# Softmax denominators in four timed steps, and head-row copies of parity 1 on another queue

## The chip, the cores and the metric

The kernel runs on one core of a Trainium2 chip. The core has a matrix engine (TensorE, PE in the profile), a vector engine (VectorE, DVE), an engine for activation functions (ScalarE, ACT), a general engine (GpSimd, POOL) and a synchronisation engine (SyncE, SP) that here only issues transfers. [...] The metric is the device time of the kernel in microseconds, as the median of its runs.

## The reference, cut to what matters

The input has 2048 tokens of width 512. It is normalised once, and two branches work on the result. Branch A is attention over a dilated window: each token looks at itself and at 7 earlier tokens, two apart. It has 32 heads of width 16. Branch B mixes neighbouring tokens between two matrix products and then runs a two-layer network with a hidden width of 1376. The output joins them.

```python
def _A_ref(x, wqkv, wo):
    H = 32; Dh = D // H
    W, dil = 8, 2
    q, k, v = ...                       # x @ wqkv, split by head
    off = jnp.arange(W) * dil           # tokens s, s-2, ..., s-14
    logits = einsum("bhsd,bhswd->bhsw", q, kg) * Dh ** -0.5
    attn = softmax(masked logits)
    o = einsum("bhsw,bhswd->bhsd", attn, vg)
    return o @ wo                       # heads merged

def _B_ref(x, w1, w2, w3, w4):
    h = gelu(layernorm(x) @ w1)
    hs = shifted(h) @ w2                # quarters shifted by -1, +1, -2, +2 tokens
    x1 = x + hs
    h2 = gelu(layernorm(x1) @ w3) @ w4
    return x1 + h2

xn = layernorm(x)
out = x + _A_ref(xn) * silu(_B_ref(xn))
```

Since a token sees only tokens of its own parity, the kernel treats the even and the odd tokens as two sequences of 1024, called parity 0 and parity 1.

## The kernel before

The parts of attention and of the network are woven together. Attention runs in 9 units of up to 128 queries for each parity. `attend(n)` handles unit n (0 to 8 are parity 0, 9 to 17 are parity 1): it computes scores for its own unit, weights the values of the unit before, and calls the functions listed in `groups[n]` and `late[n]`. Between the two parities the product with w3 (line 453) runs over four chunks of 512 tokens; the product with w4 (line 473) is woven into parity 1.

The softmax weights are not divided before the product with v. Each value tile has columns of constants beside the 16 value columns of a head, so the product also gives the denominators. Three units form a run, and the results of a run are normalised together. The denominators lie on few partitions, so they take a way through DRAM: `den_d` is written, read back as `dn` over all 128 partitions, inverted, written to `rden_d`, and read back with every value repeated for the 16 rows of its head.

```python
def spread(p, lo, hi):                     # copies head rows to tiles beside mask rows
    for w in range(2):
        for e in range(2):
            for gr in range(4):
                r = 32 * gr + DH * e
                nc.sync.dma_start(                                     # line 250
                    out=(kT, qT)[w][e][r : r + DH, :, lo:hi], in_=kq[p][w][r : r + DH, :, lo:hi]
                )

def ln3_norm(c, a=0, b=TPC):               # normalises chunk c, then turns it
    ...
            nc.vector.tensor_scalar(...)                               # line 431
    nc.sync.dma_start(out=x1n_dram[...], in_=xn3)                      # line 437
    nc.sync.dma_start_transpose(out=x1nT[c], in_=x1n_dram[...])        # line 440

def weighted_out(p, u, op):
    nc.vector.tensor_copy(out=orw[p][...], in_=op[...])                # line 554, empties o_ps
    if u == runs[p][r][1] - 1:
        normalise(p, r)

def normalise(p, r):
    nc.sync.dma_start(out=den_d..., in_=orw[p][DH : P : 32]...)        # line 567
    dn = small.tile([P, n], BF16, name="dn", tag="dn")
    nc.sync.dma_start(out=dn, in_=den_d...)                            # line 573
    rrs[p, r] = (dn, rden_d)

def pack(p, r):                            # 8 copies by GpSimd        # line 581
    ...

def normalise_mid(p, r):
    nc.vector.reciprocal(out=rb, in_=dn)                               # line 592
    nc.sync.dma_start(out=rden_d..., in_=rb)                           # line 593
    ...
    nc.sync.dma_start(out=rr, in_=rden_d...to_broadcast(...))          # line 598

def normalise_end(p, r):
    nc.vector.tensor_tensor(out=oT[p]..., in0=oT[p]..., in1=rr..., op=ALU.mult)   # line 603

late[3].append(lambda: ln3_norm(0))
late[7].append(lambda: ln3_norm(1))
for p in range(2):
    for r, (_, end, _, _) in enumerate(runs[p]):        # end is 3, 6, 9
        n = p * NU + end
        if n + 1 < 2 * NU and not (p == 0 and n >= N1):
            late[n].append(lambda p=p, r=r: pack(p, r))
            late[n + 2].append(lambda p=p, r=r: normalise_mid(p, r))
            if r == 0:
                late[n + (5 if p == 0 else 4)].append(lambda p=p, r=r: normalise_end(p, r))
late[4].append(lambda: spread(1, 0, CUT))

for n in range(N1):                        # parity 0
    attend(n)
for c in range(NCH):                       # product with w3, chunk by chunk
    for a in range((NF + 1) // 2):
        w3_pair(c, a)
        if c == 0 and a == 0:
            weighted(*prev)()              # last unit of parity 0
            ln3_stats(2); ln3_norm(2)
            ln3_stats(3); ln3_norm(3)
            load_w4()
            spread(1, CUT, M)
            pack(0, 2)
        if c == 1 and a == 0:
            normalise_end(0, 1)
            normalise_mid(0, 2)
        if c == 2 and a == 0:
            normalise_end(0, 2)
for n in range(N1, 2 * NU):                # parity 1, with the product with w4
    attend(n)
...
```

Four lines of the w4 stage come up later. Line 479 (VectorE) adds the w4 result to the residual and empties its PSUM tile. Lines 499 and 503 compute and empty the next value tile, and line 524 (ScalarE) takes the exponential of the scores. In the last stage `final_tile` multiplies with wo (line 620) and joins the two branches (lines 626 and 628).

Of the kernel before, what the change touches and what calls it, by code (L numbers as in the profile page):

```python
# [15 lines left out]
def kernel(  # L16
# [14 lines left out]
    nc = tc.nc  # L31
    P = 128
    S = 2048
    D = 512
    H = 32
# [24 lines left out]
    runs = []  # L60
# [20 lines left out]
    def at(kb, n, m):  # L81
        ar, o = (arenas[0], int(kb * KB)) if kb < 164 else (arenas[1], int((kb - 176) * KB))
        return ar[:, o : o + n * m].rearrange("p (n m) -> p n m", n=n)
# [40 lines left out]
    for c in range(NCH):  # L124
        p, k = c // 2, c % 2
        n = 1 if c == 0 else 2
        for t0 in range(k * TPC, (k + 1) * TPC, n):
            nc.sync.dma_start(
                out=xn[p][:, t0 : t0 + n, :],
                in_=xv[p, t0 * P : (t0 + n) * P, :].rearrange("(i q) d -> q i d", q=P),  # L130
# [14 lines left out]
    def load_w4():  # L145
        nc.sync.dma_start(
            out=w4_sb[:, 0 : NF - 1, :],
            in_=B_w4[0 : (NF - 1) * P, :].rearrange("(ft q) n -> q ft n", q=P),
        )
        nc.sync.dma_start(out=w4_sb[0:FL, NF - 1, :], in_=B_w4[(NF - 1) * P : F, :])  # L150
# [91 lines left out]
                    out=(kT, qT)[w][e][:, :, cs], in_=mask[:, w, cs].unsqueeze(1).to_broadcast([P, ND, CH])  # L242
                )

    def spread(p, lo, hi):
        for w in range(2):
            for e in range(2):
                for gr in range(4):
                    r = 32 * gr + DH * e
                    nc.sync.dma_start(  # L250
                        out=(kT, qT)[w][e][r : r + DH, :, lo:hi], in_=kq[p][w][r : r + DH, :, lo:hi]
                    )

# [15 lines left out]
    def layer_stats(src, name, lo=0, hi=TPC):  # L269
        n = hi - lo  # L270
        st = small.tile([P, n, nc.vector.BN_STATS_DIM], F32, name=name + "s", tag=f"{name}s{n}", bufs=2)
        mv = small.tile([P, n, nc.vector.BN_AGGR_DIM], F32, name=name + "m", tag=f"{name}m{n}", bufs=8 if n == 1 else 4)
        for j in range(n):
            nc.vector.bn_stats(out=st[:, j, :], in_=src[:, lo + j, :])
            nc.vector.bn_aggr(out=mv[:, j, :], in_=st[:, j, :])  # L275
        rstd = small.tile([P, n], F32, name=name + "r", tag=f"{name}r{n}", bufs=8 if n == 1 else 4)
        rsqrt_eps(rstd, mv[:, :, 1])
        return mv, rstd
# [143 lines left out]
    def ln3_stats(c, lo=0, hi=TPC):  # L422
        p, k = c // 2, c % 2
        l3.setdefault(c, []).append((lo, hi, *layer_stats(xn[p][:, k * TPC : (k + 1) * TPC, :], "l3", lo, hi)))

    def ln3_norm(c, a=0, b=TPC):
        p, k = c // 2, c % 2
        x_c = xn[p][:, k * TPC : (k + 1) * TPC, :]
        for lo, hi, mv, rstd in l3[c]:
            for j in range(max(lo, a), min(hi, b)):  # L430
                nc.vector.tensor_scalar(
                    out=xn3[:, j, :], in0=x_c[:, j, :], scalar1=mv[:, j - lo, 0:1],
                    scalar2=rstd[:, j - lo : j - lo + 1], op0=ALU.subtract, op1=ALU.mult,
                )
        if b < TPC:
            return
        nc.sync.dma_start(
            out=x1n_dram[c * CH : (c + 1) * CH, :].rearrange("(i q) d -> q i d", q=P), in_=xn3
        )
        nc.sync.dma_start_transpose(out=x1nT[c], in_=x1n_dram[c * CH : (c + 1) * CH, :])  # L440

    def h3(c, ft, n):
# [4 lines left out]
    def w3_pair(c, a):  # L447
        pt = psa("w3_ps")
        fts = [ft for ft in (2 * a, 2 * a + 1) if ft < NF]
        for ft in fts:  # L450
            fs = P if ft < NF - 1 else FL
            for dt in range(ND):
                nc.tensor.matmul(  # L453
                    pt[:fs, ft % 2, :], lhsT=w3_sb[:, dt, ft * P : ft * P + fs], rhs=x1nT[c][:, dt, :],
                    start=(dt == 0), stop=(dt == ND - 1),
                )
        if len(fts) == 2:
            nc.scalar.activation(h3(c, 2 * a, 2), pt, AF.Gelu_apprx_tanh)  # L458
        else:
            nc.scalar.activation(h3(c, NF - 1, 1)[:FL, 0, :], pt[:FL, 0, :], AF.Gelu_apprx_tanh)  # L460
# [100 lines left out]
    rrs = {}  # L561

    def normalise(p, r):
        _, _, ra, rw = runs[p][r]
        den_d = dram.tile([8, ND * rw], BF16, name=f"den_d{p}{r}")
        rden_d = dram.tile([8, ND * rw], BF16, name=f"rden_d{p}{r}")
        nc.sync.dma_start(
            out=den_d.rearrange("(j c) x -> c j x", j=2),
            in_=orw[p][DH : P : 32].rearrange("c j s q -> c j (s q)"),
        )  # L570
        n = H * rw // P
        dn = small.tile([P, n], BF16, name="dn", tag="dn")
        nc.sync.dma_start(out=dn, in_=den_d.rearrange("h (a m) -> (h a) m", a=P // 8))
        rrs[p, r] = (dn, rden_d)

    def pack(p, r):
        _, _, ra, rw = runs[p][r]
        for jj in range(2):
            for cg in range(4):
                hh = 4 * jj + cg  # L580
                nc.gpsimd.dma_start(  # L581
                    out=oT[p][DH * hh : DH * (hh + 1), :, ra : ra + rw],
                    in_=orw[p][32 * cg : 32 * cg + DH, jj],
                )

    def normalise_mid(p, r):
        _, _, ra, rw = runs[p][r]
        n = H * rw // P
        dn, rden_d = rrs[p, r]
        rb = small.tile([P, n], BF16, name="rb", tag="rb")  # L590
        with nc.allow_low_precision("bf16 weights"):
            nc.vector.reciprocal(out=rb, in_=dn)
        nc.sync.dma_start(out=rden_d.rearrange("h (a m) -> (h a) m", a=P // 8), in_=rb)
        if p == 0 and r:
            rr = orws[r % 2][:, 0 : ND * rw]
        else:
            rr = at(rr_at[r % 2] if p else 121, 1, ND * rw)[:, 0, :]
        nc.sync.dma_start(out=rr, in_=rden_d.unsqueeze(1).to_broadcast([8, DH, ND * rw]))
        rrs[p, r] = rr

    def normalise_end(p, r):
        _, _, ra, rw = runs[p][r]
        nc.vector.tensor_tensor(  # L603
            out=oT[p][:, :, ra : ra + rw], in0=oT[p][:, :, ra : ra + rw],
            in1=rrs[p, r].rearrange("p (s q) -> p s q", s=ND), op=ALU.mult,
        )
# [56 lines left out]
    stage_t(1, 0)  # L663
    stage_t(1, 1)
    spread(0, 0, CH)
    mask_fill(1)
    ln_stats(2)
# [9 lines left out]
    for a in (2, 3):  # L677
        qk_pair(1, a)[0]()
    spread(0, CH, M)
    stage_t(2, 0)  # L680
    stage_t(2, 1)
# [22 lines left out]
    N1 = NU  # L704
# [16 lines left out]
    late = {n: [] for n in range(2 * NU + 4)}  # L721

    def st3(n, *ts):
        for t in ts:
            late[n].append(lambda t=t: ln3_stats(t // 4, t % 4, t % 4 + 1))

    st3(1, 0, 1)
    st3(2, 2, 3)
    late[3].append(lambda: ln3_norm(0))
    st3(4, 4, 5)  # L730
    st3(5, 6)
    st3(6, 7)
    late[7].append(lambda: ln3_norm(1))

    w4s = [w4_tile(t) for t in range(S // P)]
    for n in range(N1, 2 * NU):
# [10 lines left out]
    for p in range(2):  # L747
        for r, (_, end, _, _) in enumerate(runs[p]):
            n = p * NU + end
            if n + 1 < 2 * NU and not (p == 0 and n >= N1):  # L750
                late[n].append(lambda p=p, r=r: pack(p, r))
                late[n + 2].append(lambda p=p, r=r: normalise_mid(p, r))
                if r == 0:
                    late[n + (5 if p == 0 else 4)].append(lambda p=p, r=r: normalise_end(p, r))
    CUT = CH
    late[4].append(lambda: spread(1, 0, CUT))

    prev = None

# [25 lines left out]
    for c in range(NCH):  # L785
# [3 lines that stand above are left out]
                weighted(*prev)()  # L789
                prev = None  # L790
                ln3_stats(2)
                ln3_norm(2)
                ln3_stats(3)
                ln3_norm(3)
                load_w4()
                spread(1, CUT, M)
                pack(0, 2)
            if c == 1 and a == 0:
                normalise_end(0, 1)
                normalise_mid(0, 2)  # L800
            if c == 2 and a == 0:
                normalise_end(0, 2)
    load_wo()
    for k in range(2):
# [5 lines left out]
                load_xo(1, k)  # L810
    weighted(*prev)()
    pack(1, 2)
    fq = [(0, i) for i in range(8)]
    gate(8)
    gate(9)
    for t in range(10, 16):
        w4s[t](0, NF)
        final_tile(*fq.pop(0), eng=nc.gpsimd)
        gate(t)
        if t == 11:  # L820
            normalise_end(1, 1)
        if t == 13:
            normalise_mid(1, 2)
    for _ in range(2):
        final_tile(*fq.pop(0), eng=nc.gpsimd)
    for i in (0, 2, 4, 6):
# [37 lines left out]
```

## Time and profile before

| | |
|---|---|
| median of 3 runs | 227.44 us (225.14 to 228.41) |
| span of the profiled execution | 227.5 us |
| TensorE matmul busy | 205.8 us, 90% |
| VectorE busy | 133.5 us, 59% |
| ScalarE busy | 133.1 us, 59% |
| GpSimd busy | 69.4 us, 30% |
| product with w3 (line 453) | from 93.3 to 138.8 us |
| scores of parity 1 begin | 138.9 us |
| last w4 product ends | about 209 us |

A profile of this kind is read from the engine that is nearly always busy, here TensorE: a stretch in which it idles, or runs at a lower clock, is what a change can win. What ended such a stretch is found in the table of waits and in the timelines. Idle time of the other engines costs nothing by itself. A line such as `97.92 0.92 DVE L603 ...` gives the start, the duration, the engine, the line of the kernel, the operation, the tiles written and read, and in brackets the idle time before it and what ended that. Lines with `SPq` are the issues of transfers by SyncE. Transfers that one engine issues wait in one queue: when the front one waits for data, those behind it are not issued.

### The profile page before, as it was taken

Reading aid. Unit: us, or ns where it says so; the run is one execution under the profiler, and the core shown is the slowest. Engines: PE = TensorE matmul, PEld = TensorE weight load, DVE = VectorE, ACT = ScalarE, POOL = GpSimd, SP = SyncE. Lnnn points to the kernel's source line nnn. Section 1 sums busy time; section 2 is a strip of 40 time slices with the busy share of each in tenths; the row PEclk is TensorE's granted clock in tenths of the full one; section 3 lists DMA queues with packets and bytes.
Section 4 is the critical chain, followed back from the end, with each engine's and each line's share of the span. In section 5 each row is a group of like instructions: output and inputs, shape, how many; then the busy total and the mean of one; then the engine's idle time right before and its main releaser. Section 6 shows DMA issues by size and latency. Waiting matters only on the chain.

```text
span 227.5 us, 4995 instructions
## 1 busy us (share of the span) xinstructions
PE 205.8 (90%) x1999; PEld 99.6 (44%) x2028; DVE 133.5 (59%) x242; ACT 133.1 (59%) x162; POOL 69.4 (30%) x139
## 2 busy tenths in 40 slices
PE   8799999999999999939999999299999999999860
PEld 3566455444445544413444444135444544444320
DVE  5859584343969768467340000225666769799991
ACT  2397679588798987613564658428887784221000
POOL 8880532000227236002630000000070162933761
PEclk9999999999999999976999999979999999999995
DMA  5994967969006658235497945790030150401542
GB/s 146 357 331 140 275 104 199 262 102 262 22 0 154 129 92 146 66 105 102 153 202 149 279 63 81 195 320 6 0 69 13 46 101 12 117 3 40 158 140 91
DMA packets 35550, 29.75 MB, mean 131 GB/s; under 512 B 12600, under 2 KB 33432, under 8 KB 35528
## 3 DMA queue, kind: packets, MB, share of 16 engines
q1 hardware_dynamic: 32904, 26.29, 45.4%
q0 software_dynamic: 1536, 2.10, 5.1%
q10 hardware_dynamic: 1088, 1.05, 1.4%
q8 instruction: 16, 0.26, 0.5%
q14 instruction: 6, 0.05, 0.1%
HBM read 12.39 MB, written 4.46 MB: 74 GB/s over the span
## 4 chain that ended last, share of the span: by engine, by line
PE 65%; DMA 10%; DVE 7%; issue 7%; ACT 4%; POOL 3%; SPq 1%; DVEq 0%; ACTq 0%; POOLq 0%
PE w_ps L473 15%; PE w_ps L453 8%; PE qk_ps L362 8%; PE w_ps L391 6%; PE v_ps L499 6%; PE s_ps L519 6%; PE w_ps L414 4%; DMA den_d<-orw 4%; PE qk_ps L378 3%; PE o_ps L542 3%; PE wo_ps L620 3%; ACT arena L524 3%; DVE arena L626 2%; DMA arena<-x1n_dram 2%; DMA rden_d<-rb 2%
## 5 line engine op out<-in xcount | busy, mean ns | idle before, releaser
L524 ACT ACTIVATE arena<-s_ps 128x960 bf16<-128x960 f32 (+2 forms) x72 | 63.1, 934 | 21.5 <-PE s_ps L519 15.1
L581 POOL DMA_DIRECT2D arena<-orw x48 | 24.7, 523 | 71.4 <-DVE orw L554 60.3
L473 PE MATMUL w_ps<-arena 128*128 128x512 bf16 (+1 forms) x154 | 39.4, 385 | 0.7 <-issue 0.2
L458 ACT ACTIVATE arena<-w_ps 128x1024 bf16<-128x1024 f32 x20 | 20.5, 1024 | 22.7 <-PE w_ps L453 22.0
L453 PEld LDWEIGHTS <-arena 128*128 128x128 bf16 (+1 forms) x176 | 18.1, 103 | 26.8 <-issue 7.5
L473 PEld LDWEIGHTS <-arena 128*128 128x128 bf16 (+1 forms) x176 | 16.8, 99 | 20.2 <-issue 1.8
L453 PE MATMUL w_ps<-arena 128*128 128x512 bf16 (+1 forms) x86 | 22.3, 416 | 3.7 <-DVE orw L554 3.6
L499 PE MATMUL v_ps<-wv_sb,arena 128*128 128x512 bf16 (+1 forms) x71 | 19.2, 390 | 4.4 <-DVE arena L479 4.2
L489 DVE SCALAR_TENSOR_TENSOR arena<-sig,arena 128x512 bf16<-128x512 bf16 x16 | 14.7, 926 | 14.2 <-ACT sig L488 14.1
L453 PE MATMUL w_ps<-arena,arena 128*128 128x512 bf16 (+1 forms) x86 | 19.2, 379 | 0.6 <-DMA arena<-x1n_dram 0.4
L554 DVE CAST orw<-o_ps 128x960 bf16<-128x960 f32 (+2 forms) x18 | 19.6, 1091 | 0.0
L488 ACT ACTIVATE sig<-arena 128x512 bf16<-128x512 bf16 x16 | 10.1, 629 | 16.2 <-DVE arena L479 16.2
L519 PEld LDWEIGHTS <-arena 32*128 32x128 bf16 (+1 forms) x576 | 11.8, 94 | 16.7 <-issue 15.8
L418 DVE TENSOR_TENSOR arena<-w_ps,arena 128x512 bf16<-128x512 f32 x16 | 11.0, 688 | 13.6 <-PE w_ps L414 13.6
L266 POOL TENSOR_SCALAR l3r<-l3m 128x1 f32<-128x1 f32 (+1 forms) x10 | 2.2, 224 | 54.9 <-DVE l3m L275 54.9
L519 PE MATMUL s_ps<-arena 32*128 32x120 bf16 (+2 forms) x576 | 18.5, 211 | 0.5 <-ACT arena L524 0.2
L603 DVE TENSOR_TENSOR arena<-arena,orw 128x1440 bf16<-128x1440 bf16 (+1 forms) x2 | 1.7, 836 | 29.0 <-DMA orw<-rden_d 29.0
L362 PE MATMUL qk_ps<-arena 128*128 128x512 bf16 (+1 forms) x95 | 18.2, 343 | 0.2
L628 POOL TENSOR_TENSOR arena<-arena 128x512 bf16<-128x512 bf16 x12 | 14.8, 1244 | 11.8 <-DVE arena L626 10.7
L414 PE MATMUL w_ps<-arena 128*128 128x512 bf16 x55 | 15.6, 381 | 0.6 <-issue 0.2
L503 DVE CAST v_aug<-v_ps 128x512 bf16<-128x512 f32 (+1 forms) x18 | 12.4, 686 | 5.1 <-PE v_ps L499 5.1
L391 PE MATMUL w_ps<-arena 128*128 128x512 bf16 x61 | 14.3, 379 | 0.2
(82 smaller groups left out, 263.4 us busy)
## 6 DMA issues: line engine op xcount, KB each, us to landing
arena<-arena SPq DMA_DIRECT2D x8, 512.0 KB, 6.0
arena<-arena SPq DMA_DIRECT2D x64, 64.0 KB, 2.9
x1n_dram<-arena SPq DMA_DIRECT2D x4, 512.0 KB
arena<-in_A_x_dram SPq DMA_DIRECT2D x4, 512.0 KB, 8.8
arena<-in_A_x_dram SPq DMA_DIRECT2D x6, 256.0 KB, 7.1
arena<-in_B_w_dram SPq DMA_DIRECT2D x1, 1376.0 KB
arena<-in_B_w_dram SPq DMA_DIRECT2D x1, 1280.0 KB
arena<-in_A_wqkv_dram SPq DMA_DIRECT2D x2, 512.0 KB
```

The lines of the kernel that those rows point to most:

```text
L362: nc.tensor.matmul(pt[:, b, hh * w : (hh + 1) * w], lhsT=wqk_sb[:, dt, nt * P : (nt + 1) * P], rhs=xnT[p][:, dt, k * CH + hh * w : k * CH ...
L391: nc.tensor.matmul(pt[:, b, :], lhsT=w1_sb[:, dt, g * P : (g + 1) * P], rhs=xn2T[c][:, dt, :], start=(dt == 0), stop=(dt == ND - 1),)
L414: nc.tensor.matmul(pt, lhsT=w2_src(p, g, m0), rhs=w2_sb[:, g, :], start=(g == 0), stop=(g == ND - 1))
L453: nc.tensor.matmul(pt[:fs, ft % 2, :], lhsT=w3_sb[:, dt, ft * P : ft * P + fs], rhs=x1nT[c][:, dt, :], start=(dt == 0), stop=(dt == ND - 1),)
L458: nc.scalar.activation(h3(c, 2 * a, 2), pt, AF.Gelu_apprx_tanh)
L473: nc.tensor.matmul(pt, lhsT=h3(c, ft, 1)[:fs, 0, jj * P : (jj + 1) * P], rhs=w4_sb[:fs, ft, :], start=(ft == 0), stop=(ft == NF - 1),)
L499: nc.tensor.matmul(vp[:nk, :], lhsT=xnT[p][:, dt, k0 : k0 + nk], rhs=wv_sb[:, dt, :], start=(dt == 0), stop=(dt == ND - 1),)
L519: nc.tensor.matmul(st[:nk, b, i * nq : (i + 1) * nq], lhsT=kT[e][r : r + 32, dt, k0 : k0 + nk], rhs=qT[e][r : r + 32, dt, q0 : q0 + nq], s ...
L524: nc.scalar.activation(prv[:nk, 2 * h : 2 * h + 2], st[:nk, :, 0 : 4 * nq], AF.Exp, scale=SCALE)
L554: nc.vector.tensor_copy(out=orw[p][:, :, :, q0 - ra : q0 - ra + nq], in_=op[:, :, 0 : 4 * nq].rearrange("p j (s q) -> p j s q", q=nq),)
L581: nc.gpsimd.dma_start(out=oT[p][DH * hh : DH * (hh + 1), :, ra : ra + rw], in_=orw[p][32 * cg : 32 * cg + DH, jj],)
L628: eng.tensor_tensor(out=x_o, in0=sg, in1=x_o, op=ALU.add)
```

## The change

The way of the denominators is split into four functions instead of three around the transfers: `normalise` only writes `den_d`, `normalise_dn` reads it back, `normalise_mid` inverts and writes `rden_d`, and `normalise_rr` reads that back repeated. In the same way `ln3_norm` loses its store and its transposed load to `ln3_store` and `ln3_turn`. This lets the program place each issue at a point where its data should already be there, so that the queue of SyncE and VectorE do not stand waiting. Calls that belonged to the last units of parity 0 move into the w3 stage, in a new order. The first half of the head-row copies of parity 1 (`spread(1, 0, CUT)`) moves from SyncE to GpSimd, in two lots of 8.

```diff
-    def spread(p, lo, hi):
-        for w in range(2):
+    def spread(p, lo, hi, q=nc.sync, ws=(0, 1)):
+        for w in ws:
...
-                    nc.sync.dma_start(
+                    q.dma_start(
...
+        ln3_store(c)
+
+    def ln3_store(c):
         nc.sync.dma_start(
             out=x1n_dram[...], in_=xn3
         )
+
+    def ln3_turn(c):
         nc.sync.dma_start_transpose(out=x1nT[c], in_=x1n_dram[...])
...
+        rrs[p, r] = [den_d, rden_d]
+
+    def normalise_dn(p, r):
...
-        nc.sync.dma_start(out=dn, in_=den_d...)
-        rrs[p, r] = (dn, rden_d)
+        nc.sync.dma_start(out=dn, in_=rrs[p, r][0]...)
+        rrs[p, r][0] = dn
...
+    def normalise_rr(p, r):
+        dn, rden_d = rrs[p, r]
...
-    late[3].append(lambda: ln3_norm(0))
+    late[3] += [lambda: ln3_norm(0), lambda: normalise_dn(0, 0), lambda: ln3_turn(0)]
...
-    late[7].append(lambda: ln3_norm(1))
+    late[7] += [lambda: ln3_norm(1), lambda: normalise_dn(0, 1), lambda: ln3_turn(1)]
...
                 late[n].append(lambda p=p, r=r: pack(p, r))
-                late[n + 2].append(lambda p=p, r=r: normalise_mid(p, r))
-                if r == 0:
-                    late[n + (5 if p == 0 else 4)].append(lambda p=p, r=r: normalise_end(p, r))
+                if p:
+                    late[n].append(lambda p=p, r=r: normalise_dn(p, r))
+                if n < 6 or n > N1:
+                    late[n + 2].append(lambda p=p, r=r: normalise_mid(p, r))
+                    late[n + 2].append(lambda p=p, r=r: normalise_rr(p, r))
+                if p and r == 0:
+                    late[n + 4].append(lambda p=p, r=r: normalise_end(p, r))
-    late[4].append(lambda: spread(1, 0, CUT))
+    for w in range(2):
+        late[4 + w].append(lambda w=w: spread(1, 0, CUT, nc.gpsimd, (w,)))
...
                 ln3_stats(2)
                 ln3_norm(2)
+                normalise_dn(0, 2)
+                ln3_turn(2)
+                normalise_end(0, 0)
+                normalise_mid(0, 1)
                 ln3_stats(3)
                 ln3_norm(3)
+                normalise_rr(0, 1)
+                ln3_turn(3)
                 load_w4()
+                pack(0, 2)
+                normalise_mid(0, 2)
+                normalise_rr(0, 2)
                 spread(1, CUT, M)
-                pack(0, 2)
-            if c == 1 and a == 0:
+            if c == 2 and a == 0:
                 normalise_end(0, 1)
-                normalise_mid(0, 2)
-            if c == 2 and a == 0:
                 normalise_end(0, 2)
...
     pack(1, 2)
+    normalise_dn(1, 2)
...
             normalise_mid(1, 2)
+            normalise_rr(1, 2)
```

More of the change, by code (lines that the diff above doesn't have):

```diff
@@ L570, in normalise @@
         )
-        n = H * rw // P
+        rrs[p, r] = [den_d, rden_d]
+    def normalise_dn(p, r):
+        n = H * runs[p][r][3] // P
         dn = small.tile([P, n], BF16, name="dn", tag="dn")
-        nc.sync.dma_start(out=dn, in_=den_d.rearrange("h (a m) -> (h a) m", a=P // 8))
-        rrs[p, r] = (dn, rden_d)
+        nc.sync.dma_start(out=dn, in_=rrs[p, r][0].rearrange("h (a m) -> (h a) m", a=P // 8))
+        rrs[p, r][0] = dn
     def pack(p, r):
@@ L593, in normalise_mid @@
         nc.sync.dma_start(out=rden_d.rearrange("h (a m) -> (h a) m", a=P // 8), in_=rb)
+    def normalise_rr(p, r):
+        _, _, ra, rw = runs[p][r]
+        dn, rden_d = rrs[p, r]
         if p == 0 and r:
```

## The prediction

> **What bounds the kernel now.** I read the page first. TensorE is busy 90% of the span, so time can come only from where it is idle or slow. The rows of 40 slices (5.69 us each) show where: the granted clock dips in slices 18, 19 and 27, that is 96.7 to 108.1 and 147.9 to 153.6 us.
>
> ```profile
> PEclk9999999999999999976999999979999999999995
> ```
>
> Busy time by stretch, around the two dips. The columns are start:end, length, busy us of each engine with the number of instructions, granted clock, DMA share, GB/s.
>
> ```profile
> core 0: us, PE busy (x) PEld busy (x) DVE busy (x) ACT busy (x) POOL busy (x), PEclk, DMA share, GB/s
> 96.80:100.90 4.10, 0.52 (x4) 0.12 (x3) 2.17 (x4) 1.02 (x1) 0.00 (x0) 0.84 0.43 139
> 100.90:106.40 5.50, 5.50 (x14) 1.87 (x14) 3.87 (x11) 1.02 (x1) 1.28 (x2) 0.50 0.51 103
> 143.50:147.70 4.20, 0.02 (x1) 0.03 (x2) 1.38 (x2) 1.94 (x2) 0.00 (x0) 0.96 0.86 241
> 147.70:151.50 3.80, 3.58 (x13) 1.27 (x17) 0.69 (x1) 0.00 (x0) 0.00 (x0) 0.59 1.08 364
> ```
>
> Each dip is a pair: TensorE idle for about 4 us, then busy at half the clock (0.50), at 14 matmuls in 5.5 us. The table of waits names what ended each idle stretch:
>
> ```profile
> PE v_ps L499 <- DVE arena L479: 4.2, 1, 4.2
> ...
> PE w_ps L453 <- DVE orw L554: 3.6, 1, 3.6
> ```
>
> Neither VectorE instruction was slow. The timeline of VectorE shows what stood ahead of them (start, duration, in brackets the wait before):
>
> ```profile
> 97.92 0.92 DVE L603 TENSOR_TENSOR arena<-arena,arena 128x1472 bf16<-128x1472 bf16 x1 [3.75 <-DMA arena<-rden_d]
> 99.65 0.72 DVE L592 RECIPROCAL rb<-dn 128x90 bf16<-128x90 bf16 x1 [0.81 <-DMA dn<-den_d]
> 100.28 0.56 DVE L554 CAST orw<-o_ps 128x448 bf16<-128x448 f32 x1
> ...
> 146.25 0.78 DVE L603 TENSOR_TENSOR arena<-arena,orw 128x1184 bf16<-128x1184 bf16 x1 [29.03 <-DMA orw<-rden_d]
> 146.95 0.68 DVE L479 TENSOR_TENSOR arena<-w_ps,arena 128x512 bf16<-128x512 f32 x1
> ```
>
> VectorE stood at a normalisation step waiting for a transfer, and the PSUM eviction that TensorE needed was behind it. The transfers were late because the SyncE queue, which issues them all in order, was issuing head-row copies (L250):
>
> ```profile
> 76.93 12.15 SPq L250 DMA_DIRECT2D arena<-arena  x16
> 89.18 0.54 SPq L593 DMA_DIRECT2D rden_d<-rb  x1
> 92.68 0.69 SPq L598 DMA_DIRECT2D arena<-rden_d  x1
> 93.47 0.56 SPq L567 DMA_DIRECT2D den_d<-orw  x1
> 98.04 0.33 SPq L573 DMA_DIRECT2D dn<-den_d  x1
> ...
> 124.87 14.58 SPq L250 DMA_DIRECT2D arena<-arena  x16
> 139.55 0.52 SPq L593 DMA_DIRECT2D rden_d<-rb  x1
> 141.73 0.66 SPq L598 DMA_DIRECT2D orw<-rden_d  x1
> ```
>
> So the bound is TensorE, plus two bubbles made by order in the SyncE queue and, through it, in VectorE.
>
> **What the skill says.** "TensorE: Matmul & The Clock Gate", Part 1, says that an idle window of about 3.4 us drops the array to half clock and that a similar stretch of work restores it. The trace agrees in kind: idle of 3.6 and 4.2 us, then clock 0.50 for 5.5 us and 0.59 mean over 3.8 us. The same page ("Architectural detail") calls VectorE's queue a strict FIFO; the evictions behind the waiting L603 agree. "DMA: Bandwidth & Descriptors", "Issuing engines are not separate DMA queues", says that issuing from another engine saves only sequencer time. Sequencer time and its order are what is short here: the queue spends 12.15 us on 16 issues. The engines' share over those 12 us, 0.76, is not full, but it is high enough that the copies may not get shorter by being moved. "SBUF — State Buffer", "Who interferes with whom", warns that GpSimd's descriptor writing can be locked out by some VectorE operations. In this trace 8 GpSimd copies (L581) took 4.12 us at 84.72 beside a working VectorE, so no large effect is to be seen.
>
> **The change part by part.**
>
> 1. Copies of parity 1, columns 0 to 511, leave SyncE for GpSimd, in two lots of 8. A lot costs GpSimd 8 x 0.52 = 4.1 us (estimate from the L581 row: 48 in 24.7 us busy, mean 523 ns). Lot one fits from about 75.5, when the norm helpers of late[4] end, to 79.7; lot two from about 80.8 to 85. GpSimd's next duties (the L266 at 83.90, the pack at 84.72) slip by 1 to 1.5 us; the pack then ends near 90.3. The norm of chunk 1 starts on VectorE at 89.19 and needs only the L266/L267 results, so it does not slip. The first scores that read these columns are at 138.9. Cost on the path: 0. SyncE gets 12.15 us back, at 77 to 89.
>
> 2. The order at the end of parity 0. In the old late[8] VectorE had the multiply (0,0) and the reciprocal (0,1) ahead of the last parity-0 eviction. In the new order both come after the stats and norm of chunk 2, so the eviction runs when o_ps is ready, about 95.5, and ends at 96.1. The third pair of L453 matmuls would start at 97.3, as the first two pairs end, instead of 100.90: 3.58 us saved. With no long idle the clock stays up: 5.5 us at half clock do what takes 2.75 at full, so 2.75 us more. Sum 6.3.
>
> 3. Do the next inputs keep up? Chunk 0 of L453 now ends near 93.28 + 9.66 + 0.4 = 103.3 (9.66 is chunk 1 undisturbed; 0.4 the 32 o_ps matmuls between). Chunk 1's input: norm done 90.6, store issued at once instead of at 98.47, landed 3.1 us later (the x1n_dram piece of the chain), transposed load 5.3 us (same chain): 99.0. Slack 4. Chunk 2: eviction 96.1, four stats 3.4 us as at 100.76 to 104.04, GpSimd 1.4, norm 1.4: 102.4. Then 3.1 + 5.3: about 110.9, against a need at 113.0. Slack 2. Before, it was late: the L440 load began only at 114.40, since SyncE stood 4.06 us on den_d ahead of the store, and TensorE waited 0.45 us at 119.75. That 0.45 goes too. Chunk 3: 102.4 + multiply 0.92 + reciprocal 0.72 + stats, helpers and norm 6.2 = 110.3; store, load: about 119 to 120; need at 122.6. Slack 3. Stage end about 132.2 instead of 138.85: 6.7 saved so far.
>
> 4. The multiplies (0,1) and (0,2) are in chunk 2, and the reciprocal and return load of (0,2) precede the second spread. The return load of (0,2) is issued near 119.5 and lands by 124 or 125 (issue to use took 4.5 us at 141.73). L603 is then done seven or more us before the L479 eviction, near 135.5. The wait of 4.2 us goes. From 138.85 to 151.45 TensorE took 12.6 us; its pieces at full clock are 0.65 scores, 3.56, 0.44 scores, 0.97 v_ps and 1.4 of w_ps: 7.0. ScalarE must reload its table (1.28) and run 2 x 1.94 of exponentials inside these 7.0, which just fits. Saved: 5.6, of which 4.2 are the wait and the rest is half clock.
>
> 5. The dn loads of parity 1 move behind pack in program order. Pack is on GpSimd and dn on SyncE, and at 166 to 200 us SyncE is nearly empty. Cost 0. The tail from 211.7 (15.8 us) is untouched.
>
> Sum: 6.7 + 5.6 = 12.3 us. From the median of 227.44: 215.1. I choose 215.0.
>
> **The rivals.**
>
> - *A new wait for x1nT takes the place.* Chunk 2 has slack of only 2 us, and the broadcast return loads (360 KB) now run beside the stores. For it: den_d, a small transfer, took over 4 us at 93.47 and 106.85, so traffic stretches things. Against it: SyncE is otherwise empty there. If the load is 3 us late, 1 us is lost, and 3 or 4 if an idle stretch brings the half clock back: 216 to 219.
> - *GpSimd becomes the brake.* If a copy with 1 KB pieces costs 1 us instead of 0.52, the last L266 moves to about 94, the norm of chunk 1 with it, and its input to about 103, just at need; a VectorE waiting for it also holds the eviction at 95. I would expect 217 to 221. For it: the DMA share of 0.76 during the old issues. Against it: the pack copies have rows of similar size, and all ran at about 0.52.
> - *The clock is granted by more than idleness.* If long dense work at 93 to 190 us is throttled otherwise, the 2.75 and 1.4 us of clock do not come back: 219. Against it: 109.6 to 143.5 ran dense at 1.00.
> - *The second bubble moves.* If w4, the copies and the return load share the DMA engines badly (share 0.86 at 119.7 to 129.3), L603 could still be late. It would need 10 us of delay. Unlikely.
>
> **Range and chances.** The times before spread over 3.3 us, which alone is about plus or minus 1.7 on the result. A loss of 1 to 3 us by the first rival is more likely than a gain beyond the sum. So 212.6 to 218.6. A gain under 2% would need over 222.9, meaning that both bubbles mostly stay: 0.04. Slower by 2% would need an error in my reading of the order: 0.01.
>
> **What would show it.** PEclk at 9 through slices 10 to 37 of the span; no wait of L453 on L554 and none of L499 on L479 over 1 us; L603 outside the path; the two lots of L250 as GpSimd issues at about 75 to 86 us of about 4 us each; L453 finished near 132 and the tail starting near 199. Wrong: an L453 wait on the x1n_dram load over 1 us, an L266 wait that holds the chunk-1 norm, or a half-clock stretch after 93 us.

## The result and the profile after

The changed kernel takes 217.98 us (median of 4 runs, 217.96 to 218.2) and the kernel before 227.93 (4 runs, 225.14 to 228.55). The ratio is 0.9605, 95% interval 0.9516 to 0.9693. The times of the kernel before spread over 3.4 us, those of the changed kernel over 0.24. Side by side in a later session, with more runs, the changed kernel took 217.95 us (6 runs) and the kernel before 225.99 (27 runs, 223.16 to 229.3): ratio 0.9655, interval 0.9607 to 0.9704, a gain of 8.0 us. The ratios leave out the longest executions of the kernel before, so they are not quotients of these medians; its 17 runs within 1.5% of the fastest have a median of 224.83, which makes the gain 6.9 us. In the session of the order-alone run below it had 225.0 (11 runs). The prediction was a gain of 12.3 or 12.4.

In the row of granted clock both dips are gone:

```profile
PEclk9999999999999999999999999999999999999995
```

Busy time by stretch (columns as in the prediction): chunk 0 of the w3 product, chunks 1 to 3, and the start of the w4 stage up to the next unit's scores.

```profile
core 0: us, PE busy (x) PEld busy (x) DVE busy (x) ACT busy (x) POOL busy (x), PEclk, DMA share, GB/s
93.30:103.20 9.90, 9.85 (x76) 4.60 (x76) 6.62 (x16) 5.96 (x6) 1.28 (x2) 1.00 0.34 72
103.20:131.80 28.60, 28.44 (x130) 13.10 (x131) 7.20 (x16) 16.91 (x19) 5.51 (x10) 1.00 0.76 180
131.80:138.60 6.80, 6.75 (x58) 3.07 (x58) 1.38 (x2) 5.91 (x7) 0.00 (x0) 1.00 0.69 147
```

TensorE is busy in 45.0 of these 45.3 us, at full clock. The same work took 58.2 us before (93.28 to 151.45). The line numbers have moved: the eviction of o_ps is L559, the multiply L615, the reciprocal L600, the w4 eviction L484. The timeline of VectorE in the changed kernel:

```profile
95.64 0.62 DVE L559 CAST orw<-o_ps 128x448 bf16<-128x448 f32 x1 [1.44 <-PE o_ps L547]
...
102.25 0.92 DVE L615 TENSOR_TENSOR arena<-arena,arena 128x1472 bf16<-128x1472 bf16 x1
...
103.09 0.71 DVE L600 RECIPROCAL rb<-dn 128x90 bf16<-128x90 bf16 x1
...
117.03 0.91 DVE L615 TENSOR_TENSOR arena<-arena,orw 128x1440 bf16<-128x1440 bf16 x1 [6.70 <-DMA orw<-rden_d]
...
129.28 0.78 DVE L615 TENSOR_TENSOR arena<-arena,orw 128x1184 bf16<-128x1184 bf16 x1 [11.34 <-DMA orw<-rden_d]
```

The eviction now waits only for the matmuls that fill its tile. Two multiplies still wait long for their transfers, but at a time when VectorE owes TensorE nothing. The queue of SyncE:

```profile
85.83 0.68 SPq L610 DMA_DIRECT2D arena<-rden_d  x1
86.63 0.53 SPq L572 DMA_DIRECT2D den_d<-orw  x1
90.62 0.39 SPq L440 DMA_DIRECT2D x1n_dram<-arena  x1
92.09 0.33 SPq L581 DMA_DIRECT2D dn<-den_d  x1
94.51 1.83 SPq L445 DMA_TRANSPOSE arena<-x1n_dram  x1
...
118.13 0.37 SPq L601 DMA_DIRECT2D rden_d<-rb  x1
123.68 0.65 SPq L610 DMA_DIRECT2D orw<-rden_d  x1
124.38 10.70 SPq L250 DMA_DIRECT2D arena<-arena  x16
```

So the middle of the kernel gained 12.8 us in these two profiled executions (58.2 against 45.3 us up to the next unit's scores), yet their spans differ by only 11.3 (227.5 and 216.2). The rest is at the very end. The last VectorE instruction ends 4.5 us before the end of the program in the kernel before (222.98 of 227.5) and 6.15 in the changed one (210.05 of 216.2). The closing instructions of the program (a line of the launch code; duration in ns as min/median/max, then first and last start) show what the end waits for. In the kernel before:

```profile
L859 POOLq DRAIN  x3: 40/102/5195, 221.5 to 227.2; - x3
L859 SPq DRAIN  x3: 7/7/13, 225.4 to 227.0; - x3
```

and in the changed one:

```profile
L884 POOLq DRAIN  x3: 40/102/6513, 208.6 to 215.6; - x3
L884 SPq DRAIN  x3: 7/7/13, 212.4 to 215.4; - x3
```

SyncE has seen the last store land when its first DRAIN starts (212.4), and then stands until GpSimd's long DRAIN is over: that began at 208.6 and took 6.51 us, to 215.1. It lasts 1.32 us longer than before. GpSimd has issued 64 copies here, 48 before.

### The profile page after: what moved, and what is told of

Its sections match the earlier page's. It is cut to its first block, busy times and chain, and to the rows that moved or that the text cites. A ratio compares the mean times of both kernels' runs of the same rounds, so it can differ in the third digit from the quotient of the medians.

```text
span 216.2 us, 5001 instructions
## 1 busy us (share of the span) xinstructions
PE 202.4 (94%) x1999; PEld 98.9 (46%) x2028; DVE 132.8 (61%) x242; ACT 133.1 (62%) x162; POOL 78.1 (36%) x155
## 3 DMA queue, kind: packets, MB, share of 16 engines
q0 software_dynamic: 2048, 3.15, 8.9%
q10 hardware_dynamic: 1088, 1.05, 1.4%
HBM read 12.39 MB, written 4.46 MB: 78 GB/s over the span
## 4 chain that ended last, share of the span: by engine, by line
PE 79%; DVE 5%; ACT 5%; SPq 4%; issue 4%; DMA 1%; DVEq 0%
PE w_ps L458 18%; PE w_ps L478 17%; PE qk_ps L362 7%; PE v_ps L504 6%; PE s_ps L524 6%; PE w_ps L414 5%; SPq L250 4%; PE qk_ps L378 4%; PE o_ps L547 4%; PE wo_ps L632 3%; PE w_ps L391 3%; PE warm_ps L161 3%; DVE arena L638 3%; ACT arena L529 2%; PE tr_ps L314 1%
## 5 line engine op out<-in xcount | busy, mean ns | idle before, releaser
L589 POOL DMA_DIRECT2D arena<-orw x48 | 25.2, 532 | 61.6 <-DVE orw L559 61.6
L478 PE MATMUL w_ps<-arena 128*128 128x512 bf16 (+1 forms) x154 | 38.7, 379 | 0.7 <-issue 0.2
L458 PEld LDWEIGHTS <-arena 128*128 128x128 bf16 (+1 forms) x176 | 17.5, 100 | 20.2
L478 PEld LDWEIGHTS <-arena 128*128 128x128 bf16 (+1 forms) x176 | 16.5, 97 | 19.4 <-issue 0.4
L559 DVE CAST orw<-o_ps 128x960 bf16<-128x960 f32 (+2 forms) x18 | 19.7, 1095 | 1.4 <-PE o_ps L547 1.4
L458 PE MATMUL w_ps<-arena 128*128 128x512 bf16 (+1 forms) x86 | 19.4, 379 | 0.1
L418 DVE TENSOR_TENSOR arena<-w_ps,arena 128x512 bf16<-128x512 f32 x16 | 11.0, 688 | 13.7 <-PE w_ps L414 13.6
L504 PE MATMUL v_ps<-wv_sb,arena 128*128 128x512 bf16 (+1 forms) x71 | 18.5, 381 | 0.1
L508 DVE CAST v_aug<-v_ps 128x512 bf16<-128x512 f32 (+1 forms) x18 | 12.4, 687 | 4.9 <-PE v_ps L504 4.9
L484 DVE TENSOR_TENSOR arena<-w_ps,arena 128x512 bf16<-128x512 f32 x16 | 10.9, 680 | 6.8 <-PE w_ps L478 6.7
```

Source lines behind the costliest of these rows:

```text
L458: nc.tensor.matmul(pt[:fs, ft % 2, :], lhsT=w3_sb[:, dt, ft * P : ft * P + fs], rhs=x1nT[c][:, dt, :], start=(dt == 0), stop=(dt == ND - 1),)
L478: nc.tensor.matmul(pt, lhsT=h3(c, ft, 1)[:fs, 0, jj * P : (jj + 1) * P], rhs=w4_sb[:fs, ft, :], start=(ft == 0), stop=(ft == NF - 1),)
L504: nc.tensor.matmul(vp[:nk, :], lhsT=xnT[p][:, dt, k0 : k0 + nk], rhs=wv_sb[:, dt, :], start=(dt == 0), stop=(dt == ND - 1),)
L559: nc.vector.tensor_copy(out=orw[p][:, :, :, q0 - ra : q0 - ra + nq], in_=op[:, :, 0 : 4 * nq].rearrange("p j (s q) -> p j s q", q=nq),)
L589: nc.gpsimd.dma_start(out=oT[p][DH * hh : DH * (hh + 1), :, ra : ra + rw], in_=orw[p][32 * cg : 32 * cg + DH, jj],)
```

## The experiments

Theory: two orders caused the two bubbles; how much they cost differs between executions; and GpSimd's closing DRAIN grows with its copies, so the moved copies cost 1.3 to 1.6 us at the end. The rivals are named with each run.

**The kernel before once more.** No edit.

> The kernel before, unchanged, profiled once more. Theory: the execution that the prediction was read from (device time 229.28 us for a span of 227.5) was longer than its median, 227.44, because the half-clock stretch behind each bubble has no fixed length; so this profile shows the same two waits (VectorE eviction behind a normalisation step, 3.6 and 4.2 us) and a span between 223.5 and 227.5 us, with the difference in the stretches at half clock. Rival: the bubbles themselves differ in length from run to run by over 1 us, because the transfers do.

The span was 225.9 us (device time 227.68), so 1.6 less. TensorE's timeline, matmuls only, in this execution:

```profile
100.49 7.58 PE L453 MATMUL w_ps<-arena 128*128 128x512 bf16 x28 [3.15 <-DVE orw L554]
107.90 9.66 PE L453 MATMUL w_ps<-arena,arena 128*128 128x512 bf16 x43
119.31 9.67 PE L453 MATMUL w_ps<-arena,arena 128*128 128x512 bf16 x43 [1.74 <-DMA arena<-x1n_dram]
...
146.35 1.02 PE L499 MATMUL v_ps<-wv_sb,arena 128*128 128x512 bf16 x3 [3.31 <-DVE arena L479]
147.21 2.30 PE L473 MATMUL w_ps<-arena 128*128 128x512 bf16 x6
149.44 0.61 PE L519 MATMUL s_ps<-arena 32*128 32x120 bf16 x16
```

and in the first profile:

```profile
100.90 8.91 PE L453 MATMUL w_ps<-arena 128*128 128x512 bf16 x28 [3.58 <-DVE orw L554]
109.65 9.66 PE L453 MATMUL w_ps<-arena,arena 128*128 128x512 bf16 x43
119.75 9.67 PE L453 MATMUL w_ps<-arena,arena 128*128 128x512 bf16 x43 [0.45 <-DMA arena<-x1n_dram]
...
147.68 0.58 PE L499 MATMUL v_ps<-wv_sb,arena 128*128 128x512 bf16 x1 [4.20 <-DVE arena L479]
...
151.45 0.41 PE L519 MATMUL s_ps<-arena 32*128 32x120 bf16 x16
```

The three waits differ one by one, by up to 1.3 us, as the rival has it. Their sum does not: 3.15 + 1.74 + 3.31 = 8.20 against 3.58 + 0.45 + 4.20 = 8.23. The half clock differs: from 100.49 to 107.90 is 7.41 us where the first profile has 8.75 and the undisturbed work takes 5.9 (97.3 to 103.2 in the changed kernel); from 146.35 to 149.44 is 3.09 where it has 3.77 and the undisturbed work takes 2.26. That makes 1.5 + 0.8 = 2.3 us lost at half clock against 2.85 + 1.5 = 4.4, and this 2.0 is the whole difference by the start of the second unit. In this execution the clock stayed at half beyond that point, to 151.09, so 0.4 us of the 2.0 are lost again and 1.6 remain.

Taken from the granted clock in stretches of 0.1 us, the half clock lasted from 99.59 to 106.41 and from 147.37 to 150.79 in the first profile, and from 99.89 to 103.30 and from 147.67 to 151.09 in this one. So "no fixed length" was too loose: it lasted 3.4 us, or twice that. Both profiled executions of the kernel before (229.28 and 227.68 us) are longer than its medians; one near the median was not traced, so what its bubbles cost is known only from the times.

**The order alone.** The copies go back to SyncE, still in two lots.

```diff
-        late[4 + w].append(lambda w=w: spread(1, 0, CUT, nc.gpsimd, (w,)))
+        late[4 + w].append(lambda w=w: spread(1, 0, CUT, nc.sync, (w,)))
```

> The changed kernel with its 16 moved copies back on SyncE, in the same two lots. Theory (GpSimd's closing DRAIN grows with the copies that GpSimd has issued): 48 such copies as before, so the DRAIN is 5.2 us again instead of 6.5 and the stretch from the last VectorE instruction to the end 4.5 us instead of 6.1. If the new order alone removes the bubbles, the time is 216.4 us (1.6 under 218.0). Rival (the copies must leave SyncE): the lots hold back the store of chunk 1, its transposed load starts near 97 and lands near 102.5 to 104, TensorE waits 0 to 3 us at 103 and the time is 217 to 221 us.

216.46 us (216.44 to 216.72); against the kernel before 0.9624, interval 0.9598 to 0.965. This is 1.5 us under the changed kernel, and the theory's figure within 0.1. The DRAIN was 5.197 us. The transposed load of chunk 1, and TensorE's chunks 1 and 2:

```profile
97.86 1.83 SPq L445 DMA_TRANSPOSE arena<-x1n_dram  x1
103.22 19.16 PE L458 MATMUL w_ps<-arena,arena 128*128 128x512 bf16 x86
```

The load was issued 3.35 us later than in the changed kernel, and still TensorE began chunk 1 at 103.22 without a wait. These loads landed 4.4 to 5.0 us after their issue, so 0.4 to 1 us of slack was left; the move was not needed.

**The copies alone.** The kernel before with the two lots on GpSimd.

```diff
-    late[4].append(lambda: spread(1, 0, CUT))
+    for w in range(2):
+        late[4 + w].append(lambda w=w: spread(1, 0, CUT, nc.gpsimd, (w,)))
```

> The kernel before with nothing but the 16 copies moved to GpSimd in two lots. Theory: the first bubble came from SyncE issuing these copies, so it goes (under 1 us of wait of the third matmul pair on L554 or its successor); the second, behind the other 16 copies, stays with 3 to 5 us and its half clock, and the DRAIN is 6.5 us. About 222.5 us (220.5 to 224). Rival (the order of VectorE is what matters in both): both bubbles stay, 226 us or more.

224.9 us, which misses the theory's range; ratio 0.996, interval 0.9902 to 1.0019, so no gain that can be told. Part of the theory holds: the wait on L554 is gone (the eviction ran at 95.63), the second bubble is there. But its place was taken by a new wait, which I had not counted. TensorE in this run:

```profile
103.21 9.66 PE L453 MATMUL w_ps<-arena,arena 128*128 128x512 bf16 x43
115.42 9.67 PE L453 MATMUL w_ps<-arena,arena 128*128 128x512 bf16 x43 [2.55 <-DMA arena<-x1n_dram]
...
142.70 0.58 PE L499 MATMUL v_ps<-wv_sb,arena 128*128 128x512 bf16 x1 [3.55 <-DVE arena L479]
```

and SyncE, in the old order of den_d, dn and store:

```profile
102.29 0.53 SPq L567 DMA_DIRECT2D den_d<-orw  x1
106.68 0.32 SPq L573 DMA_DIRECT2D dn<-den_d  x1
107.06 0.43 SPq L437 DMA_DIRECT2D x1n_dram<-arena  x1
110.95 2.28 SPq L440 DMA_TRANSPOSE arena<-x1n_dram  x1
```

The norm of chunk 2 was done at 102.3, but its store stood behind dn, which waited for den_d to land. With TensorE early, this wait came to the front. So in the old order the move replaces the first bubble by a shorter one at full clock and adds 1.3 us of DRAIN (6.513). This execution (225.73 us) was still 3.1 us ahead of the second profile of the kernel before at the second unit's scores (146.35 against 149.44), and 2.0 at the end; the medians show no gain. The new order gave the gain, with or without the move.

**The return load late.** The changed kernel with one step put back behind the second lot.

```diff
-                normalise_mid(0, 2)
-                normalise_rr(0, 2)
                 spread(1, CUT, M)
+                normalise_mid(0, 2)
+                normalise_rr(0, 2)
```

> The changed kernel with the inversion and return load of (0,2) put behind the second lot of 16 copies, where the kernel before had them; everything else as changed. Theory: L615 for (0,2) then waits until about 137 us, the w4 eviction L484 behind it is late and TensorE waits 1.5 to 4 us on it at the start of the w4 stage, with half clock after: 220 to 223.5 us. Rival (the early call of the multiply in the w3 stage does not matter once SyncE is free earlier): no wait over 0.5 us, 218 us.

220.16 us (219.83 to 220.36). VectorE, then TensorE in this run:

```profile
137.01 0.77 DVE L615 TENSOR_TENSOR arena<-arena,orw 128x1184 bf16<-128x1184 bf16 x1 [19.15 <-DMA orw<-rden_d]
137.71 0.68 DVE L484 TENSOR_TENSOR arena<-w_ps,arena 128x512 bf16<-128x512 f32 x1
...
138.44 1.02 PE L504 MATMUL v_ps<-wv_sb,arena 128*128 128x512 bf16 x3 [2.01 <-DVE arena L484]
```

The multiply came at 137.0, as expected, and TensorE waited 2.01 us on L484. The half clock that was expected did not follow: from the end of the wait to the next scores took 2.25 us, as undisturbed. So that order makes the second bubble: 2.2 us come back with this edit alone, of 5.7 in the first profile (4.20 of wait and 1.5 at half clock).

**The changed kernel again**, beside the kernel before on one chip.

> The changed kernel once more, beside the kernel before on one chip. Theory (the median before that the prediction started from, 227.44, was high; more executions give about 225): 218.0 us within 0.3, and a gain of 7 to 8 us rather than 10 against the kernel before. Rival (the gain is 10 or more wherever both run side by side): the kernel before at 227.5 to 228.5.

The result is given above: 217.95 and 225.99 us, so the first median of the kernel before, 227.44 from 3 runs, was 1.45 us above that of 27.

**Fewer copies by GpSimd.** The changed kernel, with the pack copies of parity 1 on SyncE.

```diff
-                nc.gpsimd.dma_start(
+                (nc.sync if p else nc.gpsimd).dma_start(
                     out=oT[p][DH * hh : DH * (hh + 1), :, ra : ra + rw],
```

> The changed kernel with the 24 pack copies of parity 1 issued by SyncE, which has little to do there; 40 copies stay on GpSimd. Theory (the closing DRAIN of GpSimd lasts about 1.2 us plus 0.082 us for each copy that GpSimd has issued): DRAIN 4.5 us instead of 6.5, span 214.2, time 216.0 us. Rival (the DRAIN waits for the last stores or for the age of the last GpSimd copy): DRAIN 6.0 to 7.0 us or unrelated to the number, time 217.5 to 218.5 us.

215.75 us (215.73 to 215.77), DRAIN 4.553 us: 2.2 us under the changed kernel, of which the DRAIN gives 1.96. The rival is out.

**The same bytes in twice the copies.** Each moved copy is cut in two.

```diff
-                    q.dma_start(out=(kT, qT)[w][e][r : r + DH, :, lo:hi], ...)
+                    for d0, d1 in ((0, 2), (2, 4)) if q is nc.gpsimd else ((0, ND),):
+                        q.dma_start(out=(kT, qT)[w][e][r : r + DH, d0:d1, lo:hi], ...)
```

> The changed kernel with each of its 16 moved copies cut in two (two of the four 128-row groups each): 32 issues by GpSimd for the same bytes and pieces, 80 GpSimd copies in all. Theory (DRAIN by the number of issues): 7.8 us. Rival (DRAIN by bytes or pieces): 6.5 us. The two lots take 7 to 8.5 us of GpSimd each, so the L266 before the norm of chunk 1 comes near 94 us. If GpSimd can become the brake, VectorE stands at that norm with evictions behind it and TensorE waits 2 to 5 us near 91 to 97: 221 to 224 us; if not, 219.3 us (only the DRAIN).

225.89 us (20 runs). The DRAIN was 7.820 us, so bytes do not set it. The time went above the range. GpSimd, then VectorE and TensorE behind it:

```profile
88.55 5.99 POOL L251 DMA_DIRECT2D arena<-arena  x12 [0.27 <-DMA arena<-arena]
94.56 0.23 POOL L267 TENSOR_SCALAR l3r<-l3m 128x1 f32<-128x1 f32 x1
```

```profile
95.48 0.41 DVE L432 TENSOR_SCALAR arena<-arena,l3m,l3r 128x512 bf16<-128x512 bf16 x1 [5.17 <-POOL l3r L268]
95.81 0.68 DVE L419 TENSOR_TENSOR arena<-w_ps,arena 128x512 bf16<-128x512 f32 x1
...
96.54 1.86 PE L379 MATMUL qk_ps<-arena 128*128 128x512 bf16 x4 [4.89 <-DVE arena L419]
```

The norm stood 5.17 us for a value that GpSimd computes after its copies, TensorE stood 4.89 us behind the eviction L419, and then ran 7 us at a mean clock of 0.58, which I had left out of the expectation. In the changed kernel the same helper ran at 86.50 and the norm at 89.22, so the margin there is some 2 us.

**The order, with few copies by GpSimd.** The order-alone kernel, plus the edit of the pack copies above.

> The new order with both lots of copies on SyncE, and also the 24 pack copies of parity 1 on SyncE; 24 copies stay on GpSimd. Theory: DRAIN 3.2 us, so that the last store and not GpSimd ends the program; span about 213.3, time 215.1 us, the fastest so far. Rival (SyncE becomes the brake at 185 us, where the load of dn for the last run stands behind 8 pack issues): L615 waits in the last stage and the time is 216 us or more.

215.14 us (215.12 to 215.18); ratio to the kernel before 0.953, interval 0.9487 to 0.9574. This is 2.8 us faster than the changed kernel.

```profile
L884 POOLq DRAIN  x3: 40/102/3235, 208.7 to 213.1; - x3
L884 SPq DRAIN  x3: 7/7/13, 212.5 to 212.8; - x3
```

The long DRAIN was over at 211.9 (208.7 and 3.24), before the last store had landed (212.5). So here, as expected, GpSimd no longer ended the program: from 40 copies to 24 the DRAIN fell by 1.32 us and the time by 0.6. The dn load of the last run moved from 186.3 to 187.1, and the reciprocal that needs it starts only at about 193.

The five sizes of the DRAIN side by side:

| copies issued by GpSimd | 24 | 40 | 48 | 64 | 80 |
|---|---|---|---|---|---|
| packets of its queue | 768 | 1280 | 1536 | 2048 | 2560 |
| MB of its queue | 1.05 | 2.10 | 2.10 | 3.15 | 3.15 |
| longest DRAIN, us | 3.24 | 4.55 | 5.20 | 6.51 | 7.82 |

Each further copy lengthens it by 0.082 us (4.585 us for 56 copies), whatever its bytes and whenever it was issued: the moved copies lie 130 us before the end. Packets grew in step, 32 for each copy, so copies and packets were not told apart.

## Why the prediction was off

1. *The copies on GpSimd (step 1).* The lots ran at 75.63 for 4.46 us and from 80.98 to 86.5, with two short waits, against 75.5 to 79.7 and 80.8 to 85. The norm did not slip. "Cost on the path: 0" holds for the middle and failed at the end: the 16 copies cost 1.3 us of DRAIN, 1.5 us of time by the order-alone run. And the 12.15 us that SyncE got back were not needed.
2. *The order at the end of parity 0 (step 2).* Right: the eviction at 95.64 (predicted 95.5), chunk 0 ended at 103.22 (103.3). The copies-alone run lost this wait as well, so either part of the change is enough for it.
3. *The next inputs (step 3).* Right: no wait of TensorE on a load; the store of chunk 3 was issued at 109.84, its transposed load at 113.55; the stage ended at 131.8 (132.2). The copies-alone run shows that the wait for x1nT, the first rival, was real in the old order.
4. *The multiplies and the second lot (step 4).* Right in kind and size: next scores at 138.64 against 151.45 before, so 12.8 us in all, where steps 3 and 4 had 12.3. The late-return run put 2.2 us of it back. The return load was slower than predicted: issued at 123.68 instead of 119.5, with L615 at 129.28 instead of about 125. From its end to the eviction L484 (135.04) 5 us were left, where the step had seven or more.
5. *Parity 1 and the tail (step 5).* "The tail is untouched" failed. The last stage was, to 0.2 us, but what follows its last instruction grew from 4.5 to 6.15 us.
6. *The sum.* The step that failed most is "From the median of 227.44: 215.1". The 12.3 us were read from an execution that took 229.28 us of device time for its 227.5 us of span, and were taken from a median of three other executions. From its own execution the sum as predicted gives 229.28 - 12.3 = 217.0; with the 12.8 and the 1.5 of the end as measured it is 218.0, the measured time. The execution was one of the long ones: its half-clock stretches cost 4.4 us, those of the second profile 2.7. For a median execution the two bubbles are worth 8.5 us, not 12.3: the kernel before took 225.0 beside the order-alone kernel's 216.46. From that comes off the 1.5 of the end. With the 27 runs, which gave a higher median, it is 8.0 us in all.

The mechanism was right and two terms were mis-sized: the bubbles, 12.3 us where a median execution had 8.5 to 9.5, and the tail, 0 where it cost 1.5. Why a median execution has smaller bubbles was not traced. The third rival (clock granted by more than idleness) is out: the clock did not fall before 211.03, after the last matmul. The second was worth more than its place: twice the copies made GpSimd the brake.

## What to carry to other kernels

Subtract what you read in a profile from the time of the execution that was profiled, and ask how far a stretch at reduced clock can vary before you carry it to a median. When a queue of transfers holds up the path, reorder and split its steps first and measure that alone; moving issues to another engine is a second change with its own bill. Look past the last computation at what the end of the program waits for.

## What the runs showed of the hardware

GpSimd's closing DRAIN took 1.27 us plus 0.082 us for each copy it had issued in the whole program (24 to 80 copies). With 40 copies or more it ended the program; with 24 the last store did.

Gaps of TensorE of 2.01 us (late return) and of 1.74 and 2.55 us (waits for x1nT: the chunk behind them took 9.50 and 9.51 us, as undisturbed) left the clock at full. Gaps of 3.15 to 4.9 us were each followed by half clock, which cost between 1.2 and 3 us.

Within an execution the granted clock changed only at points that lie a multiple of 3.41 us apart: 99.59, 106.41, 147.37, 150.79 and 222.46 in the first profile (0, 2, 14, 15 and 36 steps), 99.89, 103.30, 147.67, 151.09 and 222.77 in the second (0, 1, 14, 15 and 36). TensorE's idle time in each such step (from ends that the profile models) sorts as follows in these two traces, the changed kernel's and those of copies alone, late return and twice the copies:

| idle of TensorE within a step of 3.41 us | clock in the next step |
|---|---|
| at full clock, up to 1.95 us | full |
| at full clock, 2.01 to 3.41 us (12 steps) | half |
| at half clock, up to 0.79 us | full |
| at half clock, 0.98 and 1.31 us (before the end) | half again |

So what a gap costs depends on how it falls into the steps. The gap of 3.58 us in the first profile was followed by two steps at half clock (2.85 us lost), that of 3.15 us in the second by one (1.5 us), with the steps 0.3 us later. "TensorE: Matmul & The Clock Gate" in the Trainium skill, Part 1, gives an idle window of about 3.4 us that runs free of the program. The length agrees, but a step did not have to be idle throughout: 2.01 us of it were enough. That this makes the spread of the kernel before is likely, and not shown. It follows, as an estimate from these runs, that removing 1 us from a gap of 3.5 us can be worth more than 1 us: the gap of 3.55 us (copies alone) cost a further 1.4 us at half clock, the one of 2.55 us none.
